# Scores in 64x64 quadrants, keys transposed by DMA, whole projections and an overlapped start in a Linformer attention plus hard-swish kernel

## The chip, the cores and the metric

The kernel runs on one core of a Trainium2 chip. The metric is the device time of one launch in microseconds (us), median over several executions. PE is the TensorE matmul engine, PEld its weight loads, DVE is VectorE, ACT is ScalarE, POOL is GpSimd, SP is SyncE; SPq and POOLq are the queues on which SP and POOL issue DMAs.

## The reference, cut to what matters

```python
# q, k, v: (8 batches, 8 heads, 1024, 64); E, F: (64, 1024); w_in (512, 2048); w_out (2048, 512)
k_proj = einsum('ks,bhsd->bhkd', E, k)
v_proj = einsum('ks,bhsd->bhkd', F, v)
attn   = softmax(q @ k_proj^T / sqrt(64))          # 1024 x 64 per head
x      = (attn @ v_proj) with the heads side by side # 8192 x 512
h      = x @ w_in
out    = (h * clip(h + 3, 0, 6) / 6) @ w_out         # 8192 x 512, float32
```

So each batch has a small attention part and two large products, called the feed-forward part here. Batch b + 1's attention is woven into batch b's feed-forward part; only batch 0's has nothing to hide behind.

## The kernel before

```python
# one head pair j: two heads a = 0, 1. kb holds each head's keys twice, block-diagonally:
# the 128x128 stationary scores two blocks of 64 positions at once, half of it zeros.
def scores(self, j, qT, alloc):
    for a in range(2):
        ps = alloc()
        nc.tensor.matmul(ps, self.kb[:, 2 * j + a, :], qT[:, a, :], start=True, stop=True)
        nc.scalar.activation(self.aT[j][:, a, :], ps, AF.Exp, scale=scale)

def steps(self, qT):                    # a later batch, a piece at each yield
    ps = pat()
    for so in range(SO):                # 8
        for e in range(2):
            self.project(ps, e, every, so)
        if so % 2 == 1:
            yield                       # four pieces
    self.keys_out(ps, every); self.values_out(ps, every)
    yield; yield
    self.keys_transposed(0, H)          # 8 PE transposes, 2 copies into kb
    yield; yield
    for j in range(KO):                 # 4 head pairs
        self.scores(j, qT[:, j], pat)
        yield; yield
        den = self.sums(j)              # ones as stationary, 4 quadrant matmuls
        av = self.values(j, pat)        # values as stationary, 4 quadrant matmuls
        lns = [self.log(den[t]) for t in range(NB)]
        yield
        for t in range(NB):
            self.normalise(j, t, av[t], lns[t])   # exp(-ln), times av
            yield
# ... batch 0: by_pairs() does k projection, transposes, scores, v projection, sums, values
#     and normalise of one pair, then of the next ...
steps = Attention(b + 1, x_next).steps(q_transposed(b + 1))   # queries by DMA transpose, on SP
if b + 2 < B:
    load_kqv(b + 2)                     # 3 loads on POOL's queue; q, k, v tiles are double
```

Names: kp is the projected keys, kT the same transposed, qT the queries transposed by DMA, qTp those transposed on PE, vp the projected values, aT the exponentials of the scores.

The softmax here doesn't subtract the row's maximum and nothing guards it: scores larger than these inputs give would overflow.

Of the kernel before, what the change touches and what calls it, by code (L numbers as in the profile page):

```python
# [9 lines left out]
bf16 = mybir.dt.bfloat16  # L10
AF = mybir.ActivationFunctionType
# [4 lines left out]
def kernel(  # L16
# [11 lines left out]
    nc = tc.nc  # L28
    B, H, S, D = q.shape
    KP = E.shape[0]  # L30
    d_model = H * D
    d_ff = moe_w_in.shape[1]
    scale = 1.0 / (D ** 0.5)
    P = 128
    SO = S // P
    KO = d_model // P
    FO = d_ff // P
    TOK = 512
    NB = S // TOK
    SB = SO // NB  # L40

    kqv_dram = {
        "k": k.rearrange("b h (si so) d -> b si h so d", so=SO),
# [5 lines left out]
    out_v = out.rearrange("(b si so) m -> b si so m", si=P, so=SO)  # L49

    consts = ctx.enter_context(tc.tile_pool(name="consts", bufs=1))
    kqv_pool = ctx.enter_context(tc.tile_pool(name="kqv", bufs=2))
    qT_pool = ctx.enter_context(tc.tile_pool(name="qT", bufs=2))
    att = ctx.enter_context(tc.tile_pool(name="att", bufs=2))
# [9 lines left out]
    def pmm():  # L64
        return ps_mm.tile([P, TOK], f32, tag="mm", name="mm")
# [11 lines left out]
    ident = consts.tile([P, P], bf16, name="ident")  # L77
    make_identity(nc, ident)
    ones = consts.tile([P, D], bf16, name="ones")
    nc.vector.memset(ones, 1.0)  # L80

    kbd = [consts.tile([P, H, P], bf16, name=f"kbd{i}") for i in range(2)]
    for t in kbd:
        nc.vector.memset(t, 0.0)

    def raw_tile(name):
        return kqv_pool.tile([P, H, SO, D], bf16, tag=name, name=name)

# [1 line left out]
    kqv = {0: {n: raw_tile(n) for n in ("k", "q", "v")}}  # L90
    for j in range(KO):
        for n in ("k", "q", "v"):
            nc.gpsimd.dma_start(out=kqv[0][n][:, 2 * j:2 * j + 2],
                                in_=kqv_dram[n][0][:, 2 * j:2 * j + 2])
# [28 lines left out]
    def q_transposed(b):  # L123

        t = qT_pool.tile([P, KO, 2, TOK], bf16, tag="qT", name="qT")
        nc.sync.dma_start_transpose(t.rearrange("p j a (m n) -> p (j a m) n", n=P),
                                    kqv[b]["q"].rearrange("p h s d -> p (h s d)"))
        return t


    class Attention:
        def __init__(self, b, xT):
            self.b, self.xT = b, xT
            self.kb = kbd[b % 2]
            self.kp = att.tile([KP, H, 2, D], bf16, tag="kp", name="kp")
            self.vp = att.tile([P, H, D], bf16, tag="vp", name="vp")
            self.aT = {}


        def project(self, ps, e, hs, so):  # L140
# [14 lines left out]
        def keys_transposed(self, h0, n):  # L155
            ps = pat().bitcast(bf16)[:, :n * KP]
            for i in range(n):
                nc.tensor.transpose(ps[:, i * KP:(i + 1) * KP],  # L158
                                    self.kp[:, h0 + i].rearrange("p a d -> p (a d)"), ident[:KP, :KP])
            ps = ps.rearrange("p (h m) -> p h m", h=n)  # L160
            nc.vector.tensor_copy(self.kb[:D, h0:h0 + n, :KP], ps[:D])
            nc.vector.tensor_copy(self.kb[D:, h0:h0 + n, KP:], ps[D:])  # L162

        def scores(self, j, qT, alloc):
            self.aT[j] = att.tile([P, 2, TOK], bf16, tag="aT", name="aT")
            for a in range(2):
                ps = alloc()
                nc.tensor.matmul(ps, self.kb[:, 2 * j + a, :], qT[:, a, :], start=True, stop=True)  # L168
                nc.scalar.activation(self.aT[j][:, a, :], ps, AF.Exp, scale=scale)  # L169

        def quads(self, stationary, j, alloc):
            tiles = [alloc() for t in range(NB)]
            for t in range(NB):
                for a in range(2):
                    r, c = t * KP, a * D
                    nc.tensor.matmul(tiles[t][c:c + D], stationary(r, 2 * j + a),  # L176
                                     self.aT[j][r:r + KP, a, :], start=True, stop=True)
            return tiles

        def sums(self, j):  # L180
            return self.quads(lambda r, h: ones[r:r + KP, :], j, pat)

        def values(self, j, alloc):
            return self.quads(lambda r, h: self.vp[r:r + KP, h, :], j, alloc)

        def log(self, den):
            ln = att.tile([P, TOK], f32, tag="ln", name="ln")
            nc.scalar.activation(ln, den, AF.Ln)  # L188
            return ln

        def normalise(self, j, t, av, ln):
            rec = att.tile([P, TOK], f32, tag="rec", name="rec")
            nc.scalar.activation(rec, ln, AF.Exp, scale=-1.0)  # L193
            nc.vector.tensor_mul(self.xT[:, j, t, :], av, rec)  # L194


        def by_pairs(self):
            qt = kqv[self.b]["q"]
            for j in range(KO):
                hs = slice(2 * j, 2 * j + 2)  # L200
                pk = pat()[:, :P]
                for so in range(SO):
                    self.project(pk, 0, hs, so)
                self.keys_out(pk, hs)
                q_ps = pmm().bitcast(bf16)
                qT = att.tile([P, 2, TOK], bf16, tag="qT0", name="qT0")
                for a in range(2):
                    for m in range(SB):
                        o = (a * SB + m) * P
                        nc.tensor.transpose(q_ps[:, o:o + P],  # L210
                                            qt[:, 2 * j + a, 2 * m:2 * m + 2, :].rearrange("p s d -> p (s d)"),
                                            ident)
                    if a == 0:
                        self.keys_transposed(2 * j, 2)
                    nc.vector.tensor_copy(qT[:, a, :], q_ps[:, a * TOK:(a + 1) * TOK])  # L215
                self.scores(j, qT, pmm)
                pv = pat()[:, :P]
                for so in range(SO):
                    self.project(pv, 1, hs, so)
                self.values_out(pv, hs)  # L220
                den = self.sums(j)
                av = self.values(j, pmm)
                lns = {}
                for t in range(NB):
                    self.normalise(j, t, av[t], self.log(den[t]))


        def steps(self, qT):
            ps = pat()
            every = slice(0, H)  # L230
            for so in range(SO):
                for e in range(2):
                    self.project(ps, e, every, so)
                if so % 2 == 1:
                    yield
            self.keys_out(ps, every)
            self.values_out(ps, every)
            yield
            yield
            self.keys_transposed(0, H)  # L240
            yield
            yield
            for j in range(KO):
                self.scores(j, qT[:, j], pat)
                yield
                yield
                den = self.sums(j)
                av = self.values(j, pat)
                lns = [self.log(den[t]) for t in range(NB)]
                yield  # L250
                for t in range(NB):
                    self.normalise(j, t, av[t], lns[t])
                    yield


    def first_group(xT, t, g, fo):
# [8 lines left out]
    def second_group(b, t, g, c):  # L265
        o_ps = pmm()
        for fo in range(FO):
            nc.tensor.matmul(o_ps, g[:, fo, c * P:(c + 1) * P], w_out_sb[:, fo, :],  # L268
                             start=(fo == 0), stop=(fo == FO - 1))
            if fo % SB == SB - 1:  # L270
                yield
        o_sb = opool.tile([P, d_model], f32, tag="o_sb", name="o_sb")
        nc.scalar.copy(o_sb, o_ps)  # L273
        nc.sync.dma_start(out=out_v[b, :, NB * c + t, :], in_=o_sb)

    def x_tile():
        return xpool.tile([P, KO, NB, TOK], bf16, tag="xT", name="xT")

    xT = x_tile()
    Attention(0, xT).by_pairs()  # L280
    behind = []
    for b in range(B):
        steps = iter(())
        if b + 1 < B:
            x_next = x_tile()
            steps = Attention(b + 1, x_next).steps(q_transposed(b + 1))
        if b + 2 < B:
            load_kqv(b + 2)
        for t in range(NB):
            g = gpool.tile([P, FO, TOK], bf16, tag="g", name="g")  # L290
            for fo in range(FO):
                first_group(xT, t, g, fo)
                if b > 0 or t * FO + fo >= FO + SB + 2:
                    next(steps, None)
                if b > 0 and fo % SB == SB - 1:
                    for _ in second_group(*behind[0], fo // SB):
                        pass
                    next(steps, None)
            if b > 0:
                behind.pop(0)  # L300
            behind.append((b, t, g))
        if b == 0:
            block = behind.pop(0)
            for c in range(SB):
                for _ in second_group(*block, c):
                    next(steps, None)
        for _ in steps:
            pass
        if b + 1 < B:
            xT = x_next  # L310
# [33 lines left out]
```

## Time and profile before

| | before |
|---|---|
| time, median of 3 | 546.76 us (544.88 to 547.02) |
| profiled span | 544.9 us, mean granted clock 0.981 |
| PE busy | 516.6 us, 95% |
| one steady batch | 62.9 us |
| feed-forward part starts, in effect | 39.7 us |

The lines are in the prediction below. A page's slice is a fortieth of the span and its digit a tenth of busy time. In a timeline a PE row's length is modelled, so read a piece's cost from its start to the next piece's start. The length of a row of one DMA on SPq is the time for which it occupied SP's queue; it lands later. "Half clock" means that TensorE is granted half of its clock: 128-column transposes then start 0.107 us apart instead of 0.056. Some matmul records are missing (x15 for 16).

### The profile page before, as it was taken

The numbers are of one execution on the slowest core, as the hardware profiler recorded it, in microseconds if no ns is written. First come the engines' busy times: TensorE is split into PE (matmuls) and PEld (weight loads), VectorE is DVE, ScalarE is ACT, GpSimd is POOL, SyncE is SP. The second block draws the span as 40 slices with busy tenths as digits, with TensorE's granted clock in tenths as the row PEclk, the third lists the DMA queues.
The fourth block names the chain that finished last, engine by engine and source line by source line (L and its number), as shares of the span: only waits on it lengthen the run. The fifth ranks groups of instructions, "written<-read, shape, count | busy, mean of one in ns | idle before, by whom it ended". The sixth has DMA issues, their size and how long they took to land.

```text
span 544.9 us, 6857 instructions
## 1 busy us (share of the span) xinstructions
PE 516.6 (95%) x2597; PEld 223.0 (41%) x2648; DVE 245.3 (45%) x399; ACT 283.3 (52%) x513; POOL 34.7 (6%) x49
## 2 busy tenths in 40 slices
PE   4579988999999999999999999999999999999997
PEld 2334333344434444344443444344443444444443
DVE  2438653535435544454435444444545454333320
ACT  1456566366544774267534765356643675444421
POOL 7520010100001000100001000000000000000000
PEclk9859999999999999999999999999999999999999
DMA  8999999892048710593118900410014001110101
GB/s 130 205 207 196 186 206 231 153 222 63 38 109 145 154 40 38 110 210 86 39 41 156 210 32 28 117 40 22 37 40 116 20 38 40 39 40 38 40 38 77
DMA packets 67633, 54.18 MB, mean 99 GB/s; under 512 B 30608, under 2 KB 59280, under 8 KB 67600
## 3 DMA queue, kind: packets, MB, share of 16 engines
q0 software_dynamic: 29488, 29.63, 33.8%
q1 hardware_dynamic: 38112, 24.12, 15.3%
q8 instruction: 20, 0.33, 0.2%
q14 instruction: 13, 0.11, 0.1%
HBM read 59.24 MB, written 16.78 MB: 140 GB/s over the span
## 4 chain that ended last, share of the span: by engine, by line
PE 92%; DVE 3%; ACT 2%; issue 1%; DMA 1%; POOL 0%; ACTq 0%; POOLq 0%
PE mm L259 41%; PE mm L268 41%; PE at L141 4%; PE at L176 3%; PE at L168 2%; DMA q<-in_q_dram 1%; ACT ln L188 1%; ACT rec L193 1%; DVE qT L215 1%; DVE xT L194 1%; PE at L158 1%; PE mm L210 1%; DVE kp L148 0%; PE mm L168 0%; DVE g L263 0%
## 5 line engine op out<-in xcount | busy, mean ns | idle before, releaser
L263 DVE SCALAR_TENSOR_TENSOR g<-r,mm 128x512 bf16<-128x512 f32 x256 | 175.3, 686 | 240.4 <-ACT r L262 240.2
L259 PE MATMUL mm<-xT,w_in_sb 128*128 128x512 bf16 x997 | 238.3, 381 | 4.2 <-DVE xT L194 2.3
L268 PE MATMUL mm<-w_out_sb,g 128*128 128x512 bf16 x1002 | 229.7, 379 | 1.3 <-issue 0.2
L262 ACT ACTIVATE r<-mm 128x512 f32<-128x512 f32 x256 | 152.6, 596 | 69.7 <-PE mm L259 68.2
L268 PEld LDWEIGHTS <-g 128*128 128x128 bf16 x1024 | 99.5, 98 | 122.4 <-issue 3.7
L259 PEld LDWEIGHTS <-w_in_sb 128*128 128x128 bf16 x1024 | 95.9, 98 | 129.7 <-issue 21.9
L273 ACT COPY o_sb<-mm 128x512 f32<-128x512 f32 x64 | 37.5, 585 | 156.7 <-PE mm L268 150.3
L194 DVE TENSOR_TENSOR xT<-at,rec 128x512 bf16<-128x512 f32 x56 | 38.1, 684 | 14.3 <-ACT rec L193 14.3
L193 ACT ACTIVATE rec<-ln 128x512 f32<-128x512 f32 x64 | 39.8, 627 | 0.3
L188 ACT ACTIVATE ln<-at 128x512 f32<-128x512 f32 x64 | 35.0, 597 | 7.8 <-PE at L176 7.8
L169 ACT ACTIVATE aT<-at 128x512 bf16<-128x512 f32 x56 | 30.5, 606 | 3.0 <-PE at L168 3.0
L141 PE MATMUL at<-k,ef_t 128*64 128x512 bf16 (+1 forms) x88 | 21.8, 363 | 1.3 <-DMA k<-in_k_dram 1.3
L141 PE MATMUL at<-v,ef_t 128*64 128x512 bf16 (+1 forms) x88 | 22.3, 372 | 0.0
L100 POOL DMA_DIRECT2D q<-in_q_dram x7 | 6.2, 880 | 240.0 <-DMA qT<-q 235.5
L141 PEld LDWEIGHTS <-ef_t 128*64 128x64 bf16 x176 | 10.3, 127 | 21.4 <-issue 20.6
L168 PE MATMUL at<-qT,kbd 128*128 128x512 bf16 x56 | 16.7, 380 | 1.3 <-DVE kbd L162 1.3
L169 ACT ACTIVATE aT<-mm 128x512 bf16<-128x512 f32 x8 | 4.8, 597 | 20.4 <-PE mm L168 13.3
L153 DVE CAST vp<-at 64x512 bf16<-64x512 f32 (+1 forms) x22 | 12.1, 549 | 7.1 <-PE at L141 6.7
L176 PE MATMUL at<-aT,ones 64*64 64x512 bf16 x128 | 14.0, 429 | 0.0
L148 DVE CAST kp<-at 64x512 bf16<-64x512 f32 (+1 forms) x22 | 10.8, 529 | 1.5 <-PE at L141 1.5
L176 PE MATMUL at<-aT,vp 64*64 64x512 bf16 x112 | 10.8, 376 | 0.0
L168 PEld LDWEIGHTS <-kbd 128*128 128x128 bf16 x64 | 5.9, 104 | 9.7 <-DVE kbd L162 4.8
(33 smaller groups left out, 79.6 us busy)
## 6 DMA issues: line engine op xcount, KB each, us to landing
out_dram<-o_sb SPq DMA_DIRECT2D x64, 256.0 KB, 2.0
q<-in_q_dram POOLq DMA_DIRECT2D x7, 1024.0 KB, 10.7
k<-in_k_dram POOLq DMA_DIRECT2D x7, 1024.0 KB, 15.7
v<-in_v_dram POOLq DMA_DIRECT2D x7, 1024.0 KB, 20.6
w_in_sb<-in_moe_w_in_dram POOLq DMA_DIRECT2D x4, 512.0 KB, 13.9
w_out_sb<-in_moe_w_out_dram POOLq DMA_DIRECT2D x4, 512.0 KB, 32.7
k<-in_k_dram POOLq DMA_DIRECT2D x4, 256.0 KB, 8.1
q<-in_q_dram POOLq DMA_DIRECT2D x4, 256.0 KB, 8.7
```

The lines of the kernel that those rows point to most:

```text
L141: nc.tensor.matmul(ps[e * KP:(e + 1) * KP], ef_t[:, e, so, :], kqv[self.b]["kv"[e]][:, hs, so, :], start=(so == 0), stop=(so == SO - 1))
L168: nc.tensor.matmul(ps, self.kb[:, 2 * j + a, :], qT[:, a, :], start=True, stop=True)
L169: nc.scalar.activation(self.aT[j][:, a, :], ps, AF.Exp, scale=scale)
L176: nc.tensor.matmul(tiles[t][c:c + D], stationary(r, 2 * j + a), self.aT[j][r:r + KP, a, :], start=True, stop=True)
L188: nc.scalar.activation(ln, den, AF.Ln)
L193: nc.scalar.activation(rec, ln, AF.Exp, scale=-1.0)
L194: nc.vector.tensor_mul(self.xT[:, j, t, :], av, rec)
L259: nc.tensor.matmul(h_ps, w_in_sb[:, ko, fo * P:(fo + 1) * P], xT[:, ko, t, :], start=(ko == 0), stop=(ko == KO - 1))
L262: nc.scalar.activation(r, h_ps, AF.Relu, bias=0.5, scale=1.0 / 6.0)
L263: nc.vector.scalar_tensor_tensor(g[:, fo, :], r, 1.0, h_ps, op0=ALU.min, op1=ALU.mult)
L268: nc.tensor.matmul(o_ps, g[:, fo, c * P:(c + 1) * P], w_out_sb[:, fo, :], start=(fo == 0), stop=(fo == FO - 1))
L273: nc.scalar.copy(o_sb, o_ps)
```

## The change

Its intent: fewer mode changes and fewer matmuls per batch, and a start in which the engines overlap across head pairs. The diff is cut: left out are that output rows are stored in the new order of the tokens, and that batch 1's attention now starts with the last five groups of the second block.

```diff
-def scores(self, j, qT, alloc):
-    for a in range(2):
-        ps = alloc()
-        nc.tensor.matmul(ps, self.kb[:, 2 * j + a, :], qT[:, a, :], start=True, stop=True)
-        nc.scalar.activation(self.aT[j][:, a, :], ps, AF.Exp, scale=scale)
+def scores(self, j, alloc):
+    tiles = [alloc() for _ in range(2)]
+    for a in range(2):
+        for t in range(NB):
+            for r in range(2):          # four 64x64 quadrants: (r, t)
+                nc.tensor.matmul(tiles[r][t * KP:(t + 1) * KP, a * HT:(a + 1) * HT],
+                                 self.kT[r * D:(r + 1) * D, 2 * j + a, :],
+                                 self.qT[j][r * D:(r + 1) * D, a, t * HT:(t + 1) * HT],
+                                 start=True, stop=True)
+    for r in range(2): ...              # one Exp per tile
+def keys_transposed_dma(self):
+    nc.sync.dma_start_transpose(self.kT, self.kp.rearrange("p h a d -> p (h a d)"))
 def by_pairs(self):                    # batch 0
     for j in range(KO):
         ...                            # k projection
+        if j > 0:                      # the pair before, first block only
+            den = self.sums(j - 1, pmm, (0,))[0]
+            av = self.values(j - 1, pmm, (0,))[0]
+            rec = self.inverse(self.log(den))
         ...                            # q and key transposes, scores, v projection
+def second_block(self):                # woven into the first feed-forward block
+    for j in range(KO):
+        yield
+        ...                            # sums, values, ln, exp of block 1
 def steps(self, by_dma):
     for so in range(SO):
         for e in range(2):
             self.project(ps, e, every, so)
-        if so % 2 == 1:
-            yield
+    yield
     ...
+    if by_dma:                         # batches 2 to 7; two pairs' scores at once
+        self.keys_transposed_dma()
+        ...
+    else:                              # batch 1: queries and keys on PE
+        ...
-steps = Attention(b + 1, x_next).steps(q_transposed(b + 1))
+steps = Attention(b + 1, x_next).steps(b > 0)
```

More of the change, by code (lines that the diff above doesn't have):

```diff
@@ L40 @@
     SB = SO // NB
+    HT = TOK // 2
     kqv_dram = {
@@ L80 @@
     nc.vector.memset(ones, 1.0)
-    kbd = [consts.tile([P, H, P], bf16, name=f"kbd{i}") for i in range(2)]
-    for t in kbd:
-        nc.vector.memset(t, 0.0)
     def raw_tile(name):
@@ L133, in __init__ @@
             self.b, self.xT = b, xT
-            self.kb = kbd[b % 2]
             self.kp = att.tile([KP, H, 2, D], bf16, tag="kp", name="kp")
+            self.kT = att.tile([P, H, KP], bf16, tag="kT", name="kT")
             self.vp = att.tile([P, H, D], bf16, tag="vp", name="vp")
-            self.aT = {}
+            self.qT, self.aT = {}, {}
         def project(self, ps, e, hs, so):
@@ L159, in keys_transposed @@
                                     self.kp[:, h0 + i].rearrange("p a d -> p (a d)"), ident[:KP, :KP])
-            ps = ps.rearrange("p (h m) -> p h m", h=n)
-            nc.vector.tensor_copy(self.kb[:D, h0:h0 + n, :KP], ps[:D])
-            nc.vector.tensor_copy(self.kb[D:, h0:h0 + n, KP:], ps[D:])
-        def scores(self, j, qT, alloc):
-            self.aT[j] = att.tile([P, 2, TOK], bf16, tag="aT", name="aT")
-            for a in range(2):
-                ps = alloc()
-                nc.tensor.matmul(ps, self.kb[:, 2 * j + a, :], qT[:, a, :], start=True, stop=True)
-                nc.scalar.activation(self.aT[j][:, a, :], ps, AF.Exp, scale=scale)
@@ L171, in quads, with q_transpose @@
-        def quads(self, stationary, j, alloc):
-            tiles = [alloc() for t in range(NB)]
-            for t in range(NB):
+            nc.vector.tensor_copy(self.kT[:, h0:h0 + n, :].rearrange("p h m -> p (h m)"), ps)
+        def keys_transposed_dma(self):
+            nc.sync.dma_start_transpose(self.kT, self.kp.rearrange("p h a d -> p (h a d)"))
+        def q_transpose(self, j, alloc):
+            qt = kqv[self.b]["q"]
+            ps = alloc().bitcast(bf16)
+            for a in range(2):
+                for m in range(SB):
+                    o = (a * SB + m) * P
+                    nc.tensor.transpose(ps[:, o:o + P],
+                                        qt[:, 2 * j + a, 2 * m:2 * m + 2, :].rearrange("p s d -> p (s d)"),
+                                        ident)
+            return ps
@@ new lines, in q_out @@
+        def q_out(self, j, ps):
+            self.qT[j] = att.tile([P, 2, TOK], bf16, tag="qTp", name="qTp")
+            nc.vector.tensor_copy(self.qT[j].rearrange("p a n -> p (a n)"), ps)
+        def scores(self, j, alloc):
+            self.aT[j] = att.tile([P, 2, 2, HT], bf16, tag="aT", name="aT", bufs=KO + 1)
+            tiles = [alloc() for _ in range(2)]
[6 more added lines that the diff above has]
+                                         start=True, stop=True)
+            for r in range(2):
+                nc.scalar.activation(self.aT[j][:, r].rearrange("p a n -> p (a n)"), tiles[r],
+                                     AF.Exp, scale=scale)
@@ L174, in quads @@
+        def quads(self, stationary, j, alloc, ts=range(NB)):
+            tiles = {t: alloc() for t in ts}
+            for t in ts:
                 for a in range(2):
                     r, c = t * KP, a * D
-                    nc.tensor.matmul(tiles[t][c:c + D], stationary(r, 2 * j + a),
-                                     self.aT[j][r:r + KP, a, :], start=True, stop=True)
-            return tiles
-        def sums(self, j):
-            return self.quads(lambda r, h: ones[r:r + KP, :], j, pat)
@@ L183, in values, with sums @@
-        def values(self, j, alloc):
-            return self.quads(lambda r, h: self.vp[r:r + KP, h, :], j, alloc)
+                    nc.tensor.matmul(tiles[t][c:c + D].rearrange("p (r n) -> p r n", r=2),
+                                     stationary(r, 2 * j + a),
+                                     self.aT[j][r:r + KP, :, a, :], start=True, stop=True)
+            return tiles
+        def sums(self, j, alloc, ts=range(NB)):
+            return self.quads(lambda r, h: ones[r:r + KP, :], j, alloc, ts)
@@ L186, in log, with values @@
+        def values(self, j, alloc, ts=range(NB)):
+            return self.quads(lambda r, h: self.vp[r:r + KP, h, :], j, alloc, ts)
         def log(self, den):
@@ L189, in log, with inverse, scaled @@
             return ln
-        def normalise(self, j, t, av, ln):
+        def inverse(self, ln):
             rec = att.tile([P, TOK], f32, tag="rec", name="rec")
             nc.scalar.activation(rec, ln, AF.Exp, scale=-1.0)
+            return rec
+        def scaled(self, j, t, av, rec):
             nc.vector.tensor_mul(self.xT[:, j, t, :], av, rec)
         def by_pairs(self):
-            qt = kqv[self.b]["q"]
+            ready = None
             for j in range(KO):
@@ L204, in by_pairs @@
                 self.keys_out(pk, hs)
-                q_ps = pmm().bitcast(bf16)
-                qT = att.tile([P, 2, TOK], bf16, tag="qT0", name="qT0")
-                for a in range(2):
-                    for m in range(SB):
-                        o = (a * SB + m) * P
-                        nc.tensor.transpose(q_ps[:, o:o + P],
-                                            qt[:, 2 * j + a, 2 * m:2 * m + 2, :].rearrange("p s d -> p (s d)"),
-                                            ident)
-                    if a == 0:
-                        self.keys_transposed(2 * j, 2)
-                    nc.vector.tensor_copy(qT[:, a, :], q_ps[:, a * TOK:(a + 1) * TOK])
-                self.scores(j, qT, pmm)
+                if j > 0:
+                    den = self.sums(j - 1, pmm, (0,))[0]
+                    av = self.values(j - 1, pmm, (0,))[0]
+                    rec = self.inverse(self.log(den))
+                q_ps = self.q_transpose(j, pat)
+                self.keys_transposed(2 * j, 2)
+                self.q_out(j, q_ps)
+                self.scores(j, pmm)
+                if j > 0:
+                    self.scaled(j - 1, 0, av, rec)
                 pv = pat()[:, :P]
@@ L220, in by_pairs, with normalised, steps @@
                 self.values_out(pv, hs)
-                den = self.sums(j)
-                av = self.values(j, pmm)
-                lns = {}
-                for t in range(NB):
-                    self.normalise(j, t, av[t], self.log(den[t]))
-        def steps(self, qT):
+            den = self.sums(KO - 1, pat, (0,))[0]
+            av = self.values(KO - 1, pat, (0,))[0]
+            self.scaled(KO - 1, 0, av, self.inverse(self.log(den)))
+        def second_block(self):
+            for j in range(KO):
+                yield
+                den = self.sums(j, pat, (1,))[1]
+                av = self.values(j, pat, (1,))[1]
+                rec = self.inverse(self.log(den))
+                yield
+                self.scaled(j, 1, av, rec)
+                yield
+        def normalised(self, j):
+            den = self.sums(j, pat)
+            av = self.values(j, pat)
+            lns = [self.log(den[t]) for t in range(NB)]
+            yield
+            for t in range(NB):
+                self.scaled(j, t, av[t], self.inverse(lns[t]))
+                yield
+        def steps(self, by_dma):
+            if by_dma:
+                qT = q_transposed(self.b)
+                self.qT = {j: qT[:, j] for j in range(KO)}
             ps = pat()
@@ L233, in steps @@
                     self.project(ps, e, every, so)
-                if so % 2 == 1:
-                    yield
+            yield
             self.keys_out(ps, every)
@@ L238, in steps @@
             yield
-            yield
-            self.keys_transposed(0, H)
-            yield
-            yield
-            for j in range(KO):
-                self.scores(j, qT[:, j], pat)
+            if by_dma:
+                self.keys_transposed_dma()
+                for _ in range(6):
+                    yield
+                for j in range(0, KO, 2):
+                    self.scores(j, pat)
+                    self.scores(j + 1, pat)
+                    for _ in range(3):
+                        yield
+                    yield from self.normalised(j)
+                    yield
+                    yield from self.normalised(j + 1)
+                    yield
+            else:
                 yield
+                self.keys_transposed(0, H)
+                self.q_out(0, self.q_transpose(0, pat))
                 yield
-                den = self.sums(j)
-                av = self.values(j, pat)
-                lns = [self.log(den[t]) for t in range(NB)]
-                yield
-                for t in range(NB):
-                    self.normalise(j, t, av[t], lns[t])
+                for j in range(KO):
+                    self.scores(j, pat)
+                    if j + 1 < KO:
+                        self.q_out(j + 1, self.q_transpose(j + 1, pat))
                     yield
+                    yield from self.normalised(j)
     def first_group(xT, t, g, fo):
@@ L273, in second_group @@
         nc.scalar.copy(o_sb, o_ps)
-        nc.sync.dma_start(out=out_v[b, :, NB * c + t, :], in_=o_sb)
+        nc.sync.dma_start(out=out_v[b, :, SB * t + 2 * (c % 2) + c // 2, :], in_=o_sb)
     def x_tile():
@@ L279 @@
     xT = x_tile()
-    Attention(0, xT).by_pairs()
+    first = Attention(0, xT)
+    first.by_pairs()
+    second = first.second_block()
     behind = []
@@ L292 @@
                 first_group(xT, t, g, fo)
-                if b > 0 or t * FO + fo >= FO + SB + 2:
+                if b > 0:
+                    next(steps, None)
+                elif t == 0:
+                    next(second, None)
+                elif fo >= FO - 5:
                     next(steps, None)
```

## The prediction

> **What bounds the kernel now.** I read the page first: busy shares, the slices, the chain that ended last.
>
> ```profile
> span 544.9 us, 6857 instructions
> ...
> PE 516.6 (95%) x2597; PEld 223.0 (41%) x2648; DVE 245.3 (45%) x399; ACT 283.3 (52%) x513; POOL 34.7 (6%) x49
> ...
> PE   4579988999999999999999999999999999999997
> ...
> PEclk9859999999999999999999999999999999999999
> DMA  8999999892048710593118900410014001110101
> ...
> PE 92%; DVE 3%; ACT 2%; issue 1%; DMA 1%; POOL 0%; ACTq 0%; POOLq 0%
> ```
>
> TensorE is 92% of the chain. A slice is 13.6 us; only the first three, and two short spots later, are not full. So after the start only fewer or cheaper TensorE instructions can help; in the start a shorter chain between engines can. DVE and ACT are at about half.
>
> Next, the timeline of PE alone in a steady batch (columns: start, length, instructions):
>
> ```profile
> 157.61 1.03 PE L259 MATMUL mm<-xT,w_in_sb 128*128 128x512 bf16 x4
> 158.57 0.40 PE L141 MATMUL at<-k,ef_t 128*64 128x512 bf16 x1
> 158.57 0.40 PE L141 MATMUL at<-v,ef_t 128*64 128x512 bf16 x1
> ...
> 159.12 1.04 PE L259 MATMUL mm<-xT,w_in_sb 128*128 128x512 bf16 x4
> ...
> 168.98 0.40 PE L158 MATMUL at<-ident,kp 64*128 64x64 bf16 x8
> 169.31 1.90 PE L259 MATMUL mm<-xT,w_in_sb 128*128 128x512 bf16 x8
> 171.22 0.60 PE L168 MATMUL at<-qT,kbd 128*128 128x512 bf16 x2
> 171.66 3.62 PE L268 MATMUL mm<-w_out_sb,g 128*128 128x512 bf16 x15
> ...
> 176.07 0.41 PE L176 MATMUL at<-aT,ones 64*64 64x512 bf16 x4
> 176.31 0.39 PE L176 MATMUL at<-aT,vp 64*64 64x512 bf16 x4
> 176.63 2.76 PE L259 MATMUL mm<-xT,w_in_sb 128*128 128x512 bf16 x12
> ```
>
> Read start to start, since lengths overlap. Sixteen full matmuls take 3.45 us, so one is 0.216. A k and a v projection begin together: they share the array. Four quadrant matmuls with ones take 0.24 (176.07 to 176.31), barely more than one. Batches start every 62.9 us (windows of 157.61 to 220.50 to 283.39). Of that 256 x 0.216 = 55.3 is the feed-forward part and 7.6 is attention:
> - four projection pieces, each (159.12 - 157.61) - 4 x 0.216 = 0.65, of which 0.43 is work and 0.22 the change of array mode there and back: 2.6;
> - key transposes with their two edges and the wait before the first scores, (171.22 - 167.15) - 16 x 0.216 = 0.62;
> - four scores pairs of 0.436: 1.74;
> - four times ones and values, (176.63 - 175.12) - 0.86 = 0.65: 2.6.
>
> The start, from the timeline of 0 to 45 us:
>
> ```profile
> 17.67 0.23 PE L158 MATMUL at<-ident,kp 64*128 64x64 bf16 x2 [1.55 <-DVE kp L148]
> ...
> 25.63 0.23 PE L158 MATMUL at<-ident,kp 64*128 64x64 bf16 x2 [2.05 <-DVE kp L148]
> ...
> 40.38 4.91 PE L259 MATMUL mm<-xT,w_in_sb 128*128 128x512 bf16 x22 [0.31 <-DVE xT L194]
> ```
>
> A head pair takes 25.63 - 17.67 = 8.0 us. PE stands at the keys, whose copies queue on DVE behind the previous pair's two products with rec. Three matmuls had run before 40.38, so the feed-forward part starts in effect at 40.38 - 3 x 0.216 = 39.7.
>
> **What the Trainium skill says.** "TensorEngine Tiling (Array Packing)", Key Properties: "Changing tiling mode (not just tile) drains the TensorE". The trace agrees: full matmuls next to a projection start 0.309 apart instead of 0.216. The same section says that tiles work in parallel; the ones rows show it. "TensorE: Matmul & The Clock Gate", Part 1: the clock is half until the array has been busy about 3.4 us. PEclk agrees: 0.67 and 0.52 in 20 to 40 us, when 128-column matmuls start 0.107 apart, and 0.059 when warm. "DMA: Bandwidth & Descriptors", Issuing engines are not separate DMA queues: all transfers share 16 DMA engines. The trace agrees: the query transpose landed 5.7 us after issue in the median, but 32.2 in the worst case, amid loads.
>
> **The change, part by part.** I used the order of PE instructions of both programs.
>
> (a) Projection in one piece, batches 2 to 7: eight slots of 0.216 and one mode change, 8 x 0.216 + 0.22 = 1.95 for 2.6. Saves 0.65 a batch.
>
> (b) Keys transposed by DMA, batches 2 to 7: takes away the whole 0.62, if it lands in time. It can issue when kp is out, about 4 us after the projection ends: one more group of four (0.96), then ACT 0.60 and DVE 0.69 for it, then two copies of 0.64. The scores come 12 + 16 + 16 matmuls, 9.5 us, after the projection, so 5.5 us are free. The block is an eighth of the queries' transpose, which takes 4.1 us to issue and lands 1.6 later: by proportion about 2.2, twice that among loads. I take 0 for the steady case and set aside 1.5 us in total for late ones, mainly batch 2.
>
> (c) Scores in quadrants: 16 matmuls of 64x256 for two pairs, four at once, so four rounds of 0.107; I add 0.014 a round for starts (0.230 for 0.216 in the ones rows) and 0.19 of mode change: 0.67 for the 0.87 of two pairs. Saves 0.40 a batch.
>
> Steady sum 1.67 a batch, times six: **-10.0**.
>
> (d) Batch 0's pairs overlapped. Per pair at the half clock: scores 0.5, value projection 0.99, next keys 0.99, sums and values of one block 0.9, eight query transposes 0.86, two key transposes 0.25, then DVE copies keys (0.2) and 1024 query columns (twice 0.42) with 0.25 of handover: 5.75 us; fully warm about 4.3. The loads allow it: the w_out load that waits for the last v slice leaves at 22.9, so a pair comes every 3.9 us. First scores near 11.4 (11.2 before); fourth at 11.4 + 3 x 5.75 = 28.6; then two exps, sums, values, ln, rec and product, 4.7: 33.3, in effect 32.7 after three early matmuls; if warm, 28. PE is idle a fifth of a period, so I expect mostly the half clock: 31.2. Saves **-8.5** of 39.7. The chain at its end idles PE, so the feed-forward part should start at half clock for one window of 3.4 us, which costs **+1.7**; before, it happened to start warm.
>
> (e) Second block put off: four insertions of ones and values into the first feed-forward block. Two matmuls fill only half the array but take as long as four: 0.65 each, **+2.6**.
>
> (f) Batch 1, on PE still, and now with its queries too: projection -0.65, queries 4 x 0.55 = +2.2, scores four times 0.43 unchanged, key transposes -0.17: **+1.4**. Against it stand the stalls around it. From 64.8 to 97.8 us: 0.9 at the keys, 1.3 at the first scores, 2.0 at xT, and half a window of clock:
>
> ```profile
> 93.79 0.38 PE L259 MATMUL mm<-xT,w_in_sb 128*128 128x512 bf16 x1 [1.96 <-DVE xT L194]
> ```
>
> That one then halves the clock (0.50 in the windows view of 94.2 to 97.6), 1.7 more: 5.9 in all. Now 12 matmuls, 2.6 us, lie between the last values and the next batch, so the xT wait and its cold window should go; the keys' wait stays near 1, the first scores wait near 1 for a 1024-column copy, and each pair's exps may hold PE 0.2: 2.8. **-3.1**.
>
> Sum: -10.0 - 8.5 + 1.7 + 2.6 + 1.4 - 3.1 + 1.5 = -14.4, so 546.8 - 14.4 = 532.4; I say **532**.
>
> **Rivals.**
> 1. The key transpose by DMA becomes the new wait. For: the loads for a later batch start just after the queries' transpose has landed, beside it, and the worst landing there was 32 us. Against: the free 5.5 us, and outputs landing in 2.0 us all through. Two us a batch would give 544, within 2%.
> 2. Loads of weights and pieces are too many for quadrants: a round of 64x256 waits for its four weight loads (about 0.1 us each) instead of hiding them. For: no matmul of this size in quadrants is in the trace. Against: 128-column projections with a weight load each start 0.059 apart. At 0.2 a round, (c) turns from -0.4 to about 0 a batch: 535.
> 3. The start gets warm and follows the loads: four us earlier, and no cold window: 527.
> 4. The early start runs into the loads. w_out's last chunk waits for w_in's third, and lands near 64; its first use moves from 73 to about 70. Close, but hidden; if late, only what (d) gained is lost: 536 or so.
>
> **Range and chances.** (a) is near certain. (d) is +-4, (f) +-2, (c) -1 to +3, (b) 0 to +8 with a thin tail. Taken as independent, about +-6 around 532: **525 to 539**. Two per cent is at 535.8. Faster by over 2%: 0.75; within: 0.24; slower: 0.01.
>
> **What would show it.** (a) Full matmuls on both sides of one projection piece 1.95 + 0.86 apart for four. (b) No row "PE scores, waited for DMA kT" over 1 us; batch 2 the likeliest. (c) Two pairs' scores within 0.67 between full matmuls. (d) Key transposes 4.3 to 5.8 apart in the start; first feed-forward matmul that runs on at 28 to 33. (e) 0.65 per insertion. (f) No xT wait near 85 us and no half clock there. The steady batch should be 61.2 us instead of 62.9. Wrong if a DMA wait recurs each batch, if ACT holds PSUM buffers (two pairs' exps are 2.4 us at a stretch), or if the start stays at 8 us a pair.

## The result, and the profile after

The changed kernel took 539.97 us (median of 4, 537.72 to 540.51) against 546.01 (median of 4) of the kernel before on the same chip. The ratio is 0.9882, 95% interval 0.9845 to 0.9919: 1.2% faster, within two per cent. A ratio here is the mean time of one kernel's runs over that of the other's in the same rounds, so not quite the ratio of the medians. Executions over 1.5% slower than the fastest of the same kernel are left out of the means. The prediction was 532 with a range of 525 to 539 and 0.75 on faster by over 2%; it missed.

The page of the changed kernel, the same rows as in the prediction:

```profile
span 538.0 us, 7181 instructions
...
PE 507.5 (94%) x2774; PEld 225.3 (42%) x2824; DVE 239.3 (44%) x380; ACT 283.1 (53%) x513; POOL 34.7 (6%) x49
...
PE   4799799499999999999999999999999999999997
...
PEclk9979989989999999999999999999999999999999
DMA  8999959996119911496018911411014101111112
...
PE 90%; SPq 3%; DVE 2%; DMA 2%; issue 1%; ACT 1%; POOL 0%; ACTq 0%; POOLq 0%
```

The start fills PE earlier (4799 for 4579), but a new hole stands in the eighth slice (94 to 108 us), at a 4. The chain has a link it did not have: SPq, 3%, a DMA being issued. The DMA row has a dip in its sixth slice, to a 5, where it had 9s.

A steady batch, timeline of PE:

```profile
158.73 1.03 PE L312 MATMUL mm<-xT,w_in_sb 128*128 128x512 bf16 x4
159.68 0.40 PE L138 MATMUL at<-k,ef_t 128*64 128x512 bf16 x1
...
164.13 3.62 PE L321 MATMUL mm<-w_out_sb,g 128*128 128x512 bf16 x16
167.59 3.62 PE L312 MATMUL mm<-xT,w_in_sb 128*128 128x512 bf16 x16
171.13 0.63 PE L184 MATMUL at<-qT,kT 64*64 64x256 bf16 x16
171.70 1.47 PE L321 MATMUL mm<-w_out_sb,g 128*128 128x512 bf16 x5
```

From 158.73 to 164.13 there are sixteen full matmuls (3.45) and the projection: it costs 1.95, as predicted. From 167.59 to 171.70 there are sixteen and two pairs' scores: they cost 4.11 - 3.45 = 0.66, for 0.67 predicted. The batches in the windows 158.73 to 219.96 and 219.96 to 281.20 are 61.2 us long, as predicted. The steady part is right to a tenth of a microsecond; the miss lies before 158.7 us. Batch 2's feed-forward part began at 157.6 before and begins at 158.7 now: nothing at all is left there of the gains of the start.

The hole, in the list of PE's waits, and in the timelines of SP and of POOL:

```profile
PE at L184 <- DMA kT<-kp: 7.0, 1, 7.0
```

```profile
89.46 15.49 SPq L122 DMA_TRANSPOSE qT<-q  x1
105.07 1.20 SPq L160 DMA_TRANSPOSE kT<-kp  x1
```

```profile
79.78 0.87 POOL L96 DMA_DIRECT2D q<-in_q_dram  x1 [34.63 <-PE at L168]
```

The wait names kT, but the rows of SP show what is ahead of it. Batch 2's query transpose occupies the queue for 15.5 us, where a quiet one takes 4.1. (In the kernel before the same one already took 8.4, from 92.89, but there nothing with a deadline stood behind it.) The keys (kp is out at 94.7) wait for it until 105.07. And POOL's row tells why it is slow: the loads for batch 3 left only at 79.8, because the tile of q that they overwrite was in use until PE (L168) had transposed batch 1's last queries. They then ran beside the transpose.

After the wait the windows view shows a granted clock of 0.50 from 105.4 to 112.2, for 4.4 us of which PE had work: 2.2 us more. Together 9.2 us. It shows from end to end: batch 1's feed-forward part takes 70.5 us (88.27 to 158.73), a steady one 61.2.

### The profile page after: what moved, and what is told of

Read it like the earlier page. It is cut to its first block, busy times and chain, and to the rows that moved or that the text cites. A ratio compares the mean times of both kernels' runs of the same rounds, so it can differ in the third digit from the quotient of the medians.

```text
span 538.0 us, 7181 instructions
## 1 busy us (share of the span) xinstructions
PE 507.5 (94%) x2774; PEld 225.3 (42%) x2824; DVE 239.3 (44%) x380; ACT 283.1 (53%) x513; POOL 34.7 (6%) x49
## 4 chain that ended last, share of the span: by engine, by line
PE 90%; SPq 3%; DVE 2%; DMA 2%; issue 1%; ACT 1%; POOL 0%; ACTq 0%; POOLq 0%
PE mm L321 41%; PE mm L312 40%; PE at L198 4%; SPq L122 3%; PE at L138 3%; PE at L184 2%; DMA q<-in_q_dram 1%; PE at L168 1%; ACT aT L189 1%; DVE qTp L175 1%; DMA kT<-kp 0%; PE mm L198 0%; PE mm L184 0%; DVE g L316 0%; DVE kT L157 0%
## 5 line engine op out<-in xcount | busy, mean ns | idle before, releaser
L316 DVE SCALAR_TENSOR_TENSOR g<-r,mm 128x512 bf16<-128x512 f32 x256 | 173.3, 686 | 230.8 <-ACT r L315 230.6
L312 PE MATMUL mm<-xT,w_in_sb 128*128 128x512 bf16 x1000 | 235.3, 382 | 3.1 <-issue 2.2
L321 PE MATMUL mm<-w_out_sb,g 128*128 128x512 bf16 x998 | 232.4, 382 | 1.6 <-issue 0.4
L220 DVE TENSOR_TENSOR xT<-at,rec 128x512 bf16<-128x512 f32 x61 | 41.5, 685 | 28.4 <-ACT rec L216 28.4
L189 ACT ACTIVATE aT<-at 128x512 bf16<-128x512 f32 x56 | 29.2, 610 | 12.7 <-PE at L184 12.7
L138 PE MATMUL at<-k,ef_t 128*64 128x512 bf16 (+1 forms) x88 | 17.2, 348 | 1.6 <-DMA k<-in_k_dram 1.6
L138 PE MATMUL at<-v,ef_t 128*64 128x512 bf16 (+1 forms) x88 | 16.8, 341 | 0.0
L184 PE MATMUL at<-qT,kT 64*64 64x256 bf16 x192 | 8.0, 287 | 7.0 <-DMA kT<-kp 7.0
L184 PEld LDWEIGHTS <-kT 64*64 64x64 bf16 x256 | 6.0, 110 | 19.9 <-DMA kT<-kp 7.5
L198 PE MATMUL at<-aT,vp 64*64 64x512 bf16 x122 | 13.8, 394 | 0.0
L189 ACT ACTIVATE aT<-mm 128x512 bf16<-128x512 f32 x8 | 4.3, 594 | 14.4 <-PE mm L184 14.4
L145 DVE CAST kp<-at 64x512 bf16<-64x512 f32 (+1 forms) x22 | 10.8, 530 | 1.9 <-PE at L138 1.8
```

Source lines behind the costliest of these rows:

```text
L138: nc.tensor.matmul(ps[e * KP:(e + 1) * KP], ef_t[:, e, so, :], kqv[self.b]["kv"[e]][:, hs, so, :], start=(so == 0), stop=(so == SO - 1))
L184: nc.tensor.matmul(tiles[r][t * KP:(t + 1) * KP, a * HT:(a + 1) * HT], self.kT[r * D:(r + 1) * D, 2 * j + a, :], self.qT[j][r * D:(r + 1) ...
L189: nc.scalar.activation(self.aT[j][:, r].rearrange("p a n -> p (a n)"), tiles[r], AF.Exp, scale=scale)
L198: nc.tensor.matmul(tiles[t][c:c + D].rearrange("p (r n) -> p r n", r=2), stationary(r, 2 * j + a), self.aT[j][r:r + KP, :, a, :], start=Tr ...
L220: nc.vector.tensor_mul(self.xT[:, j, t, :], av, rec)
L312: nc.tensor.matmul(h_ps, w_in_sb[:, ko, fo * P:(fo + 1) * P], xT[:, ko, t, :], start=(ko == 0), stop=(ko == KO - 1))
```

## The experiments

Two theories at first. **Theory Q**: the query transpose crawls among late loads and the key transpose stands behind it. **Theory K**: transposing keys by DMA is itself the late thing. All runs gave correct results.

### Batch 2's keys on TensorE

```diff
-                self.keys_transposed_dma()
-                for _ in range(6): yield
+                if self.b == 2:
+                    yield; yield
+                    self.keys_transposed(0, H)
+                    for _ in range(4): yield
+                else: ...               # as it was
```

> The changed kernel, but batch 2 transposes its keys on TensorE again; its queries still come by DMA. Theory Q (the late thing is the query transpose of batch 2, which crawls for 15.5 us among the loads for batch 3; the key transpose only stands behind it on the SP queue): TensorE still idles 6 to 7 us before batch 2's first scores, now put down to DMA qT, and the time stays at 540 (539 to 541). Theory K (the key transpose by DMA is itself the late thing, as rival 1 of the prediction says): the wait of 7.0 us goes, the half clock after it too, 0.6 us of transposes comes back: 531.

Measured: 538.22 us (534.07 to 539.51), ratio 0.9847. PE's waits:

```profile
PE at L184 <- DMA qT<-q: 6.5, 1, 6.5
```

The wait stays and changes its name. Theory K is out as the main cause. One of four executions was at 534.07; no profile shows why, its mean clock (0.994) is that of another at 538.31, and it stays open.

### A tile of their own for batch 1's queries

```diff
+    q_own = consts.tile([P, H, SO, D], bf16, name="q_own")
 ...
-            kqv[b][n] = raw_tile(n)
+            kqv[b][n] = q_own if (b, n) == (1, "q") else raw_tile(n)
```

> The changed kernel with a tile of their own for batch 1's queries, so that the loads for batch 3 need not wait until TensorE has transposed the last of them (79.3 us). Theory Q: these loads leave near 45 to 62 us and are done before 80, the query transpose of batch 2 issues in 4 to 5 us and lands about 6 us after its start, the key transpose follows at about 96, no wait over 0.5 us before batch 2's scores and no half clock there: 9 us less, 531 (529 to 533). Theory K: the key transpose is late anyway; 540.

Measured: 528.79 us (528.07 to 531.81), ratio 0.9683. Timeline of SP:

```profile
90.72 4.29 SPq L124 DMA_TRANSPOSE qT<-q  x1
96.01 1.20 SPq L162 DMA_TRANSPOSE kT<-kp  x1
```

The loads for batch 3 left at 48.0, 61.2 and 62.4 us. The query transpose took 4.3 us, no wait on DMA is left before batch 2's scores, and PEclk is 1.00 there. From the ratios about 11 us come back through an edit that adds no work and removes none: theory Q holds. The wait and the half clock in the trace explain 9.2 of them; the rest is no more than these kernels' executions differ by. (The two profiled executions differ by 8.0: in this one the start ran at half clock up to 34.7 us, and batch 1's feed-forward part began 1.3 us later, at 89.5.) Windows of 75 to 80 us, of the changed kernel and of this one (time, PE, PEld, DVE, ACT, POOL, PEclk, DMA share, GB/s):

```profile
75.00:80.00 5.00, 4.85 (x41) 2.14 (x40) 1.97 (x4) 3.67 (x9) 0.22 (x1) 1.00 0.14 52
```

```profile
75.00:80.00 5.00, 4.85 (x47) 2.14 (x40) 1.98 (x3) 3.68 (x7) 0.00 (x0) 1.00 1.24 207
```

The changed kernel let the DMA engines rest at 52 GB/s just before it needed them.

### Batch 2's query transpose early

```diff
+        if b == 0:
+            early[2] = q_transposed(2)
 ...
-                qT = q_transposed(self.b)
+                qT = early.pop(self.b, None) or q_transposed(self.b)
```

> The changed kernel with the query transpose of batch 2 emitted during batch 0, as soon as its queries are there (about 60 to 70 us), so it is not in front of the key transpose; the key transpose of batch 2 then runs alone on its queue, at about 95 us, beside loads for batch 4. Theory Q: it lands within 5 us, before the scores need it at about 100.6; wait below 1 us, total 531 (529 to 533). Theory K: among loads the key transpose alone takes over 6 us; the wait is 2 us or more and the total 534 to 540.

Measured: 532.27 us (531.6 to 533.14), ratio 0.9752. The time is what theory Q said, the wait is not:

```profile
PE at L184 <- DMA kT<-kp: 2.1, 1, 2.1
```

With nothing ahead of it on its queue the key transpose issued at 95.15 in 1.2 us, but landed 8.1 us after issue, beside the loads; the quiet ones land in 2.5. So theory K is true as a smaller effect: a lone key transpose among loads overruns its 5.5 us of slack by about 2 us.

### Both blocks of batch 0 in the start

```diff
-                    den = self.sums(j - 1, pmm, (0,))[0]
-                    av = self.values(j - 1, pmm, (0,))[0]
-                    rec = self.inverse(self.log(den))
+                    den = self.sums(j - 1, pmm)          # both blocks
+                    av = self.values(j - 1, pmm)
+                    rec = [self.inverse(self.log(den[t])) for t in range(NB)]
 ...
-    second = first.second_block()
+    second = iter(())
```

> The changed kernel without putting off batch 0's second block: both blocks are summed and normalised pair by pair in the start, where four quadrant matmuls take as long as two. My account (part e of the prediction): four insertions of 0.65 us go from the feed-forward block, the start's last chain gets about 1.2 us longer (one more ln and rec on ACT), net 1 to 2 us faster than the changed kernel, 538.5. Against it (putting off pays): the start's period per pair is set by ACT and DVE, and grows by over 0.7 us a pair; 541 or more.

Measured: 533.13 us (531.84 to 534.45), ratio 0.9767, so far more than my 1 to 2 us, and faster although the wait on kT was still 7.2 us. Pairs came as fast as before the edit (key transposes at 10.5, 15.6, 20.8, 24.7): putting the block off bought nothing in the start. Batch 1's feed-forward part began at 83.2 us instead of 88.3. Of these 5.1 us, 2.6 are the four insertions; most of the rest is half clock that this kernel does not have, in the first insertions and at 68 us. I hold that the first part is caused by the edit; how much of the second is the luck of where the clock's windows fall is not settled. That the mean clock is higher in all four executions (0.990 to 0.994, against 0.981 to 0.984 of the changed kernel) speaks against luck alone.

### Both fixes, and the same again

The own tile and both blocks together.

> The changed kernel with batch 1's queries in a tile of their own and with both blocks of batch 0 done in the start. If the two gains are independent, as my account of the traces has it (9.5 us of wait and half clock at batch 2; 5 us of insertions and cold windows before it), 524 (522 to 526). If the earlier start brings the loads and batch 2's transposes together again, a wait of some us on DMA returns before batch 2's scores and the time is 528 or more.

> The same kernel as the run with both fixes, for a profile in the fast state. It was 5 us slower than two independent gains would make it. If the earlier batch 2 meets the loads again: the query transpose takes over 8 us to issue, TensorE waits 2 to 5 us on DMA before batch 2's scores, and a half clock follows. If no such wait shows, the two gains overlap elsewhere. Time 529.

Measured: 528.85 us (median of three executions, 528.39 to 530.45; ratio 0.9683), and in the repeat 529.23 (two executions, ratio 0.9687). The fourth execution of the first run, the profiled one, was slow (596.98 us, mean clock 0.852) and is not compared. The sum of gains, 524, did not come: the own tile alone was as fast. The repeat's profile shows the alternative: the query transpose issues at 83.5 and takes 10.8 us, and PE waits 2.3 us on kT, followed by a half clock of 3.4 us. The kernel had become early enough to meet the loads again.

### Batch 1's attention four groups earlier

As both fixes, with slack ahead of batch 1's key transposes and first scores:

```diff
-                elif fo >= FO - 5:
+                elif fo >= FO - 9:
 ...
-                yield                    # ahead of the key transposes
+                for _ in range(3): yield
                 self.keys_transposed(0, H)
                 self.q_out(0, self.q_transpose(0, pat))
-                yield                    # ahead of the first scores
+                for _ in range(3): yield
```

> As the run with both fixes, and batch 1's attention starts four groups earlier, with two empty steps ahead of its key transposes and two ahead of its first scores, to take away the waits of 0.9 us on DVE kp and 1.9 us on DVE qTp. If these are waits for DVE's queue, as the trace says: both gone, 2.9 us less than that run, 521. If batch 1's keys and values have not landed that early (v about 48 us, projection now near 51), a DMA wait takes their place and nothing is gained.

Measured: 528.96 us (528.53 to 530.0), ratio 0.968. The two waits, 0.9 on kp and 1.9 on qTp, did go. But no time was gained, for the reason of the run above, grown:

```profile
81.64 12.83 SPq L124 DMA_TRANSPOSE qT<-q  x1
```

PE then waited 4.4 us on kT. This points to the volume as a second bound, by an estimate: weights and four batches are about 17.0 MB as bf16 (4.2 of weights, 3.15 a batch, 0.26 for E and F), which at the 207 GB/s that the windows show is 82 us after the first load at 1 to 3 us. So by this estimate whatever asks for the DMA engines before about 85 us shares them with the loads, if those for batch 3 were let in ahead. The next run tests it, together with other edits.

### The order of the transfers mended

Both blocks, early steps, the early query transpose (the loads for batch 3 then wait for its tile of q, so they come after it), and batch 2's keys on PE; no own tile.

> Both blocks in the start, batch 1's attention four groups earlier, batch 2's query transpose early (so that the loads for batch 3 wait for it instead of standing ahead of it), batch 2's keys on TensorE. If what held the last two runs was the loads' volume (207 GB/s without a pause until 85 to 95 us, and batch 2's transposes among them), no DMA wait over 0.5 us is left before batch 2's scores and the half clock at 95 us goes: the run with early steps less 6 us, 523 (521 to 525). If batch 2's queries still land after 92 us, a wait on DMA qT stays and the time is 526 or more.

Measured: 522.84 us (521.67 to 523.52), ratio 0.9565, 95% interval 0.9545 to 0.9584: 4.4% faster than the kernel before. No wait on DMA is left before batch 2's scores, and the clock has no half window after 30 us. It is the fastest version here. POOL's row shows the new order, the first load for batch 3 leaving when the query transpose has landed:

```profile
78.14 0.87 POOL L96 DMA_DIRECT2D q<-in_q_dram  x1 [34.20 <-DMA qT<-q]
```

The same with batch 2's keys by DMA:

> As the first of these, but batch 2's keys by DMA as in the changed kernel. The lone key transpose then meets the loads for batch 3, and should land about 8 us after issue, as it did with the early query transpose (8.1 us): a wait of about 2 us and perhaps a half clock after it; 2 to 4 us slower, 526.

Measured: 527.11 us (523.58 to 527.86), ratio 0.9636, with a wait of 2.7 us on kT in its profile. The profiled execution was the one at 523.58, but it was so fast because of its start: the clock was full from 13.7 us on, and batch 1's feed-forward part began at 78.6 us, for 80.0 in the run above. From there to batch 3's feed-forward part it took 64.0 us for 61.7. So the price of the wait is 2.3 us, the 2.7 less the 0.4 of transposes not done on PE, while the clock stays up. By the ratios it is 3.9. The slower executions were not profiled; their mean clock (0.993 or 0.994, for 0.997 to 1.0 in the run above) would fit one half window more, 1.7 us.

The same with the keys of batches 2 to 7 on PE:

> The fastest kernel so far with the keys of all of batches 3 to 7 transposed on TensorE too, not only batch 2's. Part b of the prediction, isolated: eight transposes and their edges, 0.44 us, come back in five batches, 2.2 us; and the 0.17 us of wait before the first scores that the kernel before had need not come back, because more matmuls lie between now: 525. If the DMA transposes cost more than is seen (SP queue, loads put off), no slower: 523.

Measured: 525.22 us (523.88 to 525.61), ratio 0.9608. The difference of the ratios is 0.43%, 2.3 us, for five batches: 0.47 each. The traces agree: from the start of batch 3's feed-forward part to the matmuls after its first scores it is 13.41 us for 12.97. Key transposes by DMA pay where the DMA engines are quiet.

### What the overlap of batch 0's pairs alone is worth

As both fixes, with the pairs one after the other (sums, values and products of a pair ahead of the next pair's keys).

> As the run with both fixes, but batch 0's pairs one after the other: each pair's sums, values and products before the next pair's keys. It measures what the overlap alone is worth. From the traces: a pair took 8.0 us before and 5.2, 5.0, 3.8 with overlap, the feed-forward part started in effect at 39.7 and now near 29; so 8 to 10 us slower than the run with both fixes, 532 to 534. If instead DMA or the new scores set the start, less than 5.

Measured: 532.5 us (532.32 to 532.88), ratio 0.9743: 3 us slower than both fixes, not 8 to 10. In the changed kernel key transposes start at 10.16 and 15.31; in this one:

```profile
17.04 0.28 PE L157 MATMUL at<-ident,kp 64*128 64x64 bf16 x2 [1.13 <-DVE kp L147]
24.29 0.28 PE L157 MATMUL at<-ident,kp 64*128 64x64 bf16 x2 [1.13 <-DVE kp L147]
```

A serial pair takes 7.25 us, an overlapped one 5.15 at half clock and 3.84 (20.30 to 24.14) once warm. The feed-forward part starts in effect at 36.6 here (37.26, less three early matmuls) and at 28.8 in the repeat of both fixes (29.43, likewise): 7.8 us, nearly what I expected. But of these 7.8, the run with both fixes gave about 4 back: its wait of 2.3 us on kT and half a window of clock, 1.7 us, which this later kernel does not have. The rest, 3.8, is the difference of the two profiled spans (530.6 and 526.9). (For the serial case I had taken the 8.0 us pairs of the old scores.)

### The projection in one piece, alone

The kernel before, with one edit, the four empty steps kept:

```diff
                 for e in range(2):
                     self.project(ps, e, every, so)
-                if so % 2 == 1:
-                    yield
+            for _ in range(SB):
+                yield
```

> The kernel before with one edit: the projection of a batch in one piece instead of four. Part a of the prediction: three mode changes of 0.22 us less for each of seven batches, 4.6 us less, 541. Against it: the longer piece of 1.95 us makes ACT and DVE run dry and gives part of it back, 543 or more.

Measured: 541.13 us (540.71 to 542.14), ratio 0.9907: by the ratio 5.1 us less, for 4.6 expected. PE's waits have no new entry. This part by itself gives nearly four fifths of the 1.2% that the whole changed kernel shows.

## Why the prediction was wrong

**(a) Projection in one piece: right.** 1.95 us in the trace, and the run of it alone.

**(b) Keys by DMA: the step that failed.** The prediction put it so: "I take 0 for the steady case and set aside 1.5 us in total for late ones, mainly batch 2." The steady case and the place were right (no later batch waits); the size was 9.2 us, 7.0 of wait and 2.2 of half clock. The term was mis-sized because the working gave the key transpose an issue time of "about 4 us after the projection ends" and a landing of "about 2.2, twice that among loads". It took the SP queue to be free. In the trace the keys stood behind the batch's query transpose, which needed 15.5 us; with it moved away, a lone key transpose needed 8.1. (Its proportion was off too, though it cost nothing: 4.1 / 8 + 1.6 is 2.1, and a quiet one issues in 1.2 and lands after 2.5 to 2.8.) Neither load times nor tile reuse of batch 3 were worked through, though (f) had moved batch 1's queries to PE, and so the moment at which their tile is free, from the landing of their transpose to 79.3 us; the loads left at 71.4 before and at 79.8 now. And the trace of the kernel before had shown batch 2's query transpose at 8.4 us to issue, twice the 4.1 that the working used. The own tile, which removes just this dependency, gave about 11 us by the ratios.

Rival 1 named the mechanism as one that recurs in each batch and gave 544. It struck one batch, once. Rival 4 looked at the loads too, but at w_out, which PE first used at 67.7 without a wait.

**(c) Scores in quadrants: right**, 0.66 for 0.67; four rounds of 64x256 hide their weight loads, so rival 2 is out.

**(d) Overlap: better than said.** Pairs took 5.15, 4.99 and 3.84 us for 5.75 cold and 4.3 warm. Taking 44 matmuls and four insertions back from 42.96 us, where the first feed-forward block runs on alone, the start is 30.9 in effect, half clock included; 31.2 + 1.7 was predicted. Part of this is luck: the 3.84 came while the clock was full, from 20.0 to 26.9 us, and in the profile of the own tile, at half clock all through the start, the same pairs took 5.15 or 5.16. (PEclk shows full clock before 20 us, but transposes 0.107 apart say half.)

**(e) Second block put off: the cost was right**, 0.65 per insertion once warm (39.16 to 42.41 is twelve matmuls and one insertion, 3.25 - 2.59 = 0.66). That it is a cost and no gain, the run with both blocks in the start shows.

**(f) Batch 1: half right.** The wait on xT and its cold window went. But from 42.96 to 88.27 there are 148 full matmuls (32.0) and 8.6 of attention in 45.3 us, so 4.7 of stalls for 2.8 predicted: the first scores waited 1.9 rather than about 1 on the query copy, and a half clock from 67.8 to 71.2 followed that gap.

The sum: -2.0 at the start, +1.9 in batch 1, +7.7 in (b) is 7.6 us, and the span, predicted at 544.9 - 14.4 = 530.5, came out at 538.0. That accounts for the miss. The range was too narrow on one side for a reason the prediction had written down itself: the worst landing of 32.2 us amid loads was in its own text, but the thin tail of (b) stopped at 8.

## What to carry to other kernels

When a change moves where a tile is last read, follow the load that overwrites it: it leaves at another time and may meet a transfer on the critical path. Work out when the DMA engines are full by volume and rate, and put transfers with a deadline ahead of loads with none, by giving the load a later buffer to wait for. A gain in one part can make the next part early enough to run into such a queue; two gains add up only if the queue is mended too.

## What the Trainium skill lacked or had wrong

- "DMA: Bandwidth & Descriptors", Issuing engines are not separate DMA queues, calls the sequencer's issue time, of DMAs in general, "usually small relative to the DMA itself". For DMA transposes it is most of it: 4.1 us of 5.7 to landing when quiet, 15.5 of 17.7 among loads, and the next transfer on SP waits for it. It has no figure for a DMA transpose beside loads: here a small one landed in 8.1 us for 2.5 quiet, a 1 MB one in 17.7 for 5.6.
- "TensorEngine Tiling (Array Packing)", Key Properties, says that a mode change drains the array and gives no cost. Here it is 0.19 to 0.22 us for going there and back.
- "TensorE: Matmul & The Clock Gate", Part 4, gives about 390 ns for a 128x128 bf16 transpose in isolation and about 275 in a kernel, and no figure for a stream of them. The trace has rows of 220 ns (their ends are modelled), and in a stream at full clock they start 0.056 us apart, 0.107 at half clock.
